# A new order of all steps, and another choice of the steps that GpSimd takes, in a gated-attention kernel with two feed-forward layers

## The chip, the cores and the metric

The kernel runs on one core of one Trainium2 chip. The metric is the device time of one execution in microseconds (us). The engines are named as in the profile: PE is TensorE, DVE is VectorE, ACT is ScalarE, POOL is GpSimd, SP is SyncE, which here does nothing but issue DMAs.

## The reference

```python
def _attn_ref(q, k, v, f_logit):          # (4, 8, 768, 48) each
    f = 1.0 / (1.0 + np.exp(-f_logit))
    state = np.zeros((B, H, D, D))
    for t in range(S):
        state = f[:, :, t, :, None] * state + np.einsum('bhd,bhe->bhde', k[:, :, t], v[:, :, t])
        y[:, :, t] = np.einsum('bhd,bhde->bhe', q[:, :, t], state)
    return y
# x = y as 3072 tokens of 384
def _moe_ref(x, w_a, w_b, w_out):         # 384 -> 1536 -> 384
    return ((x @ w_a) * (x @ w_b)) @ w_out
def _moe2_ref(x, w1, w2, w3, w_out):      # 384 -> 768 -> 384
    h = np.maximum(np.maximum(x @ w1, x @ w2), x @ w3)
    return h @ w_out
```

All arrays are drawn in double precision for the weights and single precision for q, k, v and f_logit; the output is single precision.

## The kernel before

The 3072 tokens are cut into 12 segments of 256 (three for each batch entry). Each segment goes through three kinds of work.

1. The attention's products inside groups of eight tokens are done with elementwise steps on DVE or POOL (`direct_steps`, kind "d", lines L200 to L254, three of them reductions that only DVE does: L203, L212 and L231), with a few copies and the sigmoid on ACT (kind "c"). Then `attn_steps`: small transposes and matmuls on PE (kind "P", in this order: total, transposes of k and q, the output of the groups, state keys, state update, state read, and twice scores and scores by values), tables on DVE or POOL (kind "g", L291 to L300), scalings, state decays and gains and the masks (kind "h"), copies out of PSUM on ACT (kind "b"). `x_out` (kind "x") brings the segment's result with ten DMAs into the layout of the next layer.
2. The first layer, `moe1_steps`. Every product is made of three matmuls of a high and a low part. A step "m" is nine matmuls of 128x256 (one 128-row tile of x @ w_a or x @ w_b), a step "y" nine matmuls of the down product. After each pair of tiles ACT copies the a half out of PSUM (L479), DVE multiplies it by the b half (L483, `v_ab`), ACT rounds it (L487), DVE takes the low part (L492, `v_g`, "gl"), and then two steps "y" (L502) can run.
3. The second layer, for six blocks of 512 tokens: steps "u" (`up2`, nine matmuls of 128x512, L646), copies and maxima on ACT and DVE (kinds "N" and "M"), steps "o" (`down`, three matmuls of 128x384, L672), then a copy and a store ("O", "X").

The weights arrive as double precision and are turned into a high and a low part on the chip, unit by unit of 128x384 (`conv_steps`). There are 36 units for the first layer and 24 for the second. A unit is loaded by SP (kinds "r" and "W"), read by two ACT instructions (L544, L545), shifted by DVE (L550), added by POOL (L554, always POOL), rounded by ACT (L561) and subtracted by DVE or POOL (L566). A step "m" needs the three units of its 384 columns, a step "y" its own unit.

Nothing is scheduled by the compiler. The steps are put into queues by kind, and the string `ORDER` names, letter by letter, which kind's next step is emitted:

```python
    with tc.manual_schedule():
        todo = {kind: iter(steps) for kind, steps in queues.items()}
        for kind in ORDER or CANON:
            f, args = next(todo[kind])
            f(*args)
```

Each engine carries out its own steps in that order and waits, by semaphores, for what a step reads or overwrites. So a step that waits holds up everything behind it on its engine, and SP's DMAs too wait for each other in the order of the letters. There are 2775 letters. The steps that either engine can do are numbered (0 to 643) in the order in which they are put into the queues, and the set `ON_POOL` says which of them POOL takes; DVE does the others:

```python
    def flex(kind, f):
        e = pool if len(FLEX) in ON_POOL else vec
        FLEX.append(len(CANON))
        step(kind, f, e)
```

Of the kernel before, what the change touches and what calls it, by code (L numbers as in the profile page):

```python
# [16 lines left out]


ORDER = (
    "zqzjckzrd0drd0vdddirdddr1tddddrddrcd0dP1drr12br2ddgd3Pgcd2b3kP4jgbd0hdgdgr13dg020dgdd4qd1ggdhbrrd01b"  # L20
    "4hhgP341P0hbh1Ph2hh32hrhPc204h1ldd3dr34h2bdr2d4P030h3Pdv14dr4t10Pd23h20d1122Pbd43b01dd01xd4ddrc3xddd"
    "sd2P2bdrddd3ggcgge4dPbsrP0dde1srem20brkmgdjm34r1db4dhg0q3g2ddg1nhrbdr0g34grmh1P4f320hmnP34f0mm2yhhb"
    "Pr10n43h0m2rrh1y34fm2hmn043f0nd1m12mrhyryhh3l23c141h4f20103m2rbPhrn3m4P014fm1021rr342hn3023Pd4Pm1h2m"
    "0y23fr34y40dn11044mvf1y23d2d0d01r324ynP34b41ddx0mdmf22mdnfdmm3dxn413mdy2yf3nds4f4sedddysecebyPddnPdb"
    "mcmgdngmgdddmdgtdbknfqgmndPmfbbmhymdgnmdhdgbgdymdfnmPjchgdfhghPnbmhfymhvldPhmdnhfhmdydbdhdnhhmfhnmd"
    "dddPdPhmPdfPdhmPdcbdntmyddPxdPmddfbcgxydmmbndqdymyddPdggsdfndsggsgeeyebgfdkjmnddyYmfbybdhmchgynnPhhP"
    "mdghgdnfbmPnhfmdbhdyhdmhdhymhhnhfddmPPmnmflhPdPhvmdddndmdcyfdnmdddPmydcdfbmdtnbdPbjfPgddbmnydmdmgkc"
    "PfdhmddgdnfmymbqxmdbdyndbgdxmvfgsdYesesyyglenfnmhdyggfmgyhPPmbyhhdPdhmgnhdhnnmhdhmfbndmfymddnhhhdct"
    "ddddmPdhPfjdcqhdynmkmPfPddnmmYhddyfPdncmbfmddPddPddmnbbgdfxdbggdydmPxPggngyhbmmbbggyfhmnhhdhfPgvdbd"
    "ynmPymhgmhfhndybhdhhdhhmdslhdedyPfsnesPdefmcymyhddmdPPnmnnhddfdtmPnfdmbncddjddmPbPybhddmfcmykdgmdmnd"  # L30
    "gfnPdddgqmdgmyfddnfdbmndmddgymmymgfmxgbhdgnyfbldndhmvhmYymPxfddgddPnfmydnhbmshPfysdsdbeeenmdyhcmfgd"
    "jhdhhymhhhtyPcdPhnnmnddmPfkPdhnmfmPmnmydmfmbPnPfddndmdcmfddymdqmbyndmfndmbdgdymdfgmbyxngxmhfdngdmdf"
    "dgymvnmydYgdgmyfngddhPdcsdssePeyedblmfdybdmgnbfdjhghkymyndnPnmbmbhcPdhhdfhdnhfqhdmmhhndhhymPdPdfmdyc"
    "hmPnPddmfynmhdPbdddfdmydmdddbnmYPfPvmbddndbmgfndfdyghmmgdggPddxnPgmddyfdbbmygmmbxndydfncmsshgdfdesey"
    "eymnfcdymtjhdynhmPkmdqddcnngbddmhgfhbhnfPhmdmnhhydmmhdhhhdfPPdhlnfdmmdPPddhndmfmPdmybmPndbddYgfdvPd"
    "ngtybmgmydxPdgfyggnhdbmxyghfgbmdggbhPnPhmmhycdhmbPfmydmnhfhbydnhchshdhflhssnededePdPyhdmPfdjqdPdymy"
    "dnhmnddPmnkdYmcdddfbbxPnbddPmfbmPdgdnmgmgggfdnghbbybgmgdfdhymnhymmfnhxytdgdhmmdPgPfmdhndbfmnfdPhdvm"
    "mnymfcmyhmhhhnhdcmldymftbdhsnyedPhsfPnsyeehmyPPfymdhPymbbPPnmbnndgddmdbdfYndPmfghbmdgybgndgmmfnymdxm"
    "fyggnmmlhfbndyfmghmPPgnhxmymfyhnmmbfynmgmPfhnhyhmmfhyhnhhmshyfnebPfsshePehmymymnPnPmYhnmPfmnfbnmxym"
    "fnxmwyfmmnmfmWynWmmymfnAABmfBynWCAfBmWAnDmCymWfmnCBfWWEymAmDymCAnsDssyDfnyeBeemfymyWmWEnCnBnAmDEECDB"  # L40
    "AfWWnmCmBAWfEBmpECyADmnfWnCBmymDDEEACfWmyGGmnWmyDfEBnWfHGmWAmWACEHBnCDyBmHmDpuAuyWBNCfDAumCBnWmDfEuE"
    "nWACuMDyMmBNfEnNAACmuDMEMWAyfmnMmymByEfYCnuNBfCMDyuEABEWDyCAonDBnoBuACoDouENCMGWoAuMBEoCDNEBooAEMGuN"
    "MoHBMuDEoNCDEouCHuDGoHMoNMouuoMuNoMNoMMuooouNEMuNuMoMOoopNXuOMoGuHNXoOoMuMOoNuuGMooNMuMuouNMooHXNoMu"
    "ooGMNouMXNMuMHuoooNuoNMuoMoMuNouoMNooOuMoopOMuONuuXOMNoMouMGXoHoNuMoNMuXMuGuuNooHoNMooMoGuMoNMoXoHoN"
    "uMuMuNoMNuuoMpMGoNuoGMouooOouOYNMMNuXuouMXoNMOMouOouNoMNouMuMooNoHNMuMuoMouooNuuuMoGNHoXMHMooNuuMouX"
    "pNMoMouoNMoOouuGoONMoMOuNuMoHNOuMMGoNooMoooNuHuMMuNuuMoouoNMMuXuooNuXMoGNuXHMMoooNMNuouMXMuoooNMNuuo"
    "ouMOMoNuOouMNoOooMMONouuNMXuoMMXuNMouooNouMMoooNMouooNuMMuNouNMuooMMNooMoXOXoXoOoXOXOX"
)


ON_POOL = {
# [12 lines left out]
}  # L64

CANON = []
# [744 lines left out]
```

## Time and profile before

| what | value |
|---|---|
| median of 3 runs | 971.65 us (971.62 to 972.44) |
| the profiled execution | 970.14 us |
| its span, from the first to the last instruction | 968.4 us |
| PE, PEld (weight loads) busy | 903.6 us (93%), 837.8 us |
| DVE, ACT, POOL busy | 573.3 us, 336.0 us, 305.0 us |
| mean granted TensorE clock | 0.995 |

The profiled execution took 1.7 us more than its span, and the median of the runs lies 1.5 us above the profiled execution. PE's busy time is the union of its matmuls, so that what is missing to the span (64.8 us) is time in which no matmul ran. A busy time on DVE and POOL runs from the start of an instruction to its end, and takes in time in which the instruction was held up on the way.

### The profile page before, as it was taken

The page shows a single profiled execution, that of the slowest core. Times are in us where ns is not written, and L with a number is a line of the kernel's source. Part 1 is how long each engine was busy: PE and PEld are TensorE (multiplying, and loading weights), DVE is VectorE, ACT ScalarE, POOL GpSimd, SP SyncE. Part 2 cuts the span into 40 slices and gives each one's busy share as a digit, 9 for nine tenths or more (in the row PEclk, how much of TensorE's full clock was granted, in tenths as well). Part 3 has the DMA queues.
Part 4 walks back from the last instruction along what each step waited for, and adds up shares of the span by engine and source line. Part 5 has one row for each costly group of instructions (what it writes and reads, how often), then busy time and mean ns, then how long its engine had stood idle before and what let it go on. Part 6 is the DMA issues. An engine that isn't in the chain of part 4 may idle for free.

```text
span 968.4 us, 22900 instructions
## 1 busy us (share of the span) xinstructions
PE 903.6 (93%) x9860; PEld 837.8 (87%) x9860; DVE 573.3 (59%) x893; ACT 336.0 (35%) x640; POOL 305.0 (31%) x297
## 2 busy tenths in 40 slices
PE   1348989999999999999999999999999999999998
PEld 0338889999999999999999999999888888888887
DVE  7999988977877857678765432464522232323221
ACT  4456742423324323242342323564421212112121
POOL 3543637464365336443263300462400000000000
PEclk9999989999999999999999999999999999999999
DMA  8446021322224221231220104261110110100000
GB/s 300 153 161 273 7 78 59 123 76 71 90 64 124 67 75 34 64 119 42 78 91 18 58 2 159 80 226 45 33 44 12 44 49 20 35 28 17 1 32 34
DMA packets 36294, 74.72 MB, mean 77 GB/s; under 512 B 5344, under 2 KB 17760, under 8 KB 36192
## 3 DMA queue, kind: packets, MB, share of 16 engines
q1 hardware_dynamic: 36192, 73.25, 22.3%
q8 instruction: 77, 1.26, 0.6%
q14 instruction: 25, 0.20, 0.1%
HBM read 59.07 MB, written 9.44 MB: 71 GB/s over the span
## 4 chain that ended last, share of the span: by engine, by line
PE 85%; DVE 9%; DMA 2%; SPq 1%; issue 1%; ACT 1%; POOL 0%; DVEq 0%; ACTq 0%; POOLq 0%
PE p L646 23%; PE pb L473 15%; PE pa L473 15%; PE y L502 15%; PE y L672 4%; PE pa L672 2%; PE pb L672 2%; PE w L275 2%; PE o L395 2%; PE o L365 2%; PE w L378 2%; PE w L337 1%; DMA kn<-in_k_dram 1%; DVE gl L492 1%; DMA ub<-in_moe_w_b_dram 1%
## 5 line engine op out<-in xcount | busy, mean ns | idle before, releaser
L473 PE MATMUL pb<-xh,ub 128*128 128x256 f32 x864 | 166.0, 288 | 1.4 <-DVE ub L566 0.9
L473 PE MATMUL pa<-xh,ua 128*128 128x256 f32 x864 | 167.0, 290 | 0.0
L502 PE MATMUL y<-gh,uo 128*128 128x256 f32 x864 | 164.6, 286 | 1.5 <-ACT gh L487 0.9
L646 PE MATMUL p<-ub,u 128*128 128x512 f32 x486 | 165.9, 395 | 0.0
L502 PEld LDWEIGHTS y<-gh,uo 128*128 128x128 f32 x864 | 135.9, 193 | 3.4 <-ACT gh L487 1.1
L473 PEld LDWEIGHTS pa<-xh,ua 128*128 128x128 f32 x864 | 136.8, 195 | 2.1
L473 PEld LDWEIGHTS pb<-xh,ub 128*128 128x128 f32 x864 | 134.8, 192 | 4.4 <-DVE ub L566 1.3
L473 PE MATMUL pa<-xl,ua 128*128 128x256 f32 x432 | 123.8, 287 | 2.1 <-DVE xl L464 2.1
L502 PE MATMUL y<-gl,uo 128*128 128x256 f32 x432 | 123.4, 286 | 2.5 <-DVE gl L492 2.5
L473 PE MATMUL pb<-xl,ub 128*128 128x256 f32 x432 | 122.3, 283 | 0.0
L646 PEld LDWEIGHTS p<-ub,u 128*128 128x128 f32 x486 | 90.5, 188 | 19.1
L646 PE MATMUL p<-ua,u 128*128 128x512 f32 x324 | 101.8, 395 | 0.0
L487 ACT CAST gh<-a 128x512 fp32r<-128x512 f32 x72 | 44.6, 619 | 139.1 <-DVE a L483 118.1
L483 DVE TENSOR_TENSOR a<-a,pb 128x512 f32<-128x512 f32 x72 | 49.2, 683 | 73.1 <-PE pb L473 71.3
L473 PEld LDWEIGHTS pa<-xl,ua 128*128 128x128 f32 x432 | 84.0, 195 | 2.8 <-DVE xl L464 2.7
L502 PEld LDWEIGHTS y<-gl,uo 128*128 128x128 f32 x432 | 83.5, 193 | 3.1 <-DVE gl L492 3.1
L656 DVE TENSOR_TENSOR uo<-uo,p 128x512 f32<-128x512 f32 x36 | 24.8, 688 | 101.1 <-PE p L646 84.0
L473 PEld LDWEIGHTS pb<-xl,ub 128*128 128x128 f32 x432 | 82.9, 192 | 0.0
L479 ACT COPY a<-pa 128x512 f32<-128x512 f32 x72 | 42.5, 590 | 87.9 <-DVE gl L492 43.8
L492 DVE TENSOR_TENSOR gl<-a,gh 128x512 fp32r<-128x512 f32 x72 | 64.2, 891 | 12.8 <-ACT gh L487 12.7
L646 PEld LDWEIGHTS p<-ua,u 128*128 128x128 f32 x324 | 60.4, 188 | 11.7
L656 DVE TENSOR_TENSOR ua<-ua,p 128x512 f32<-128x512 f32 x36 | 24.8, 688 | 72.1 <-PE p L646 72.0
(206 smaller groups left out, 1558.7 us busy)
## 6 DMA issues: line engine op xcount, KB each, us to landing
vlev<-in_v_lev_dram SPq DMA_DIRECT2D x12, 576.0 KB, 4.4
u<-in_moe_w_dram SPq DMA_DIRECT2D x18, 384.0 KB, 5.4
uo<-in_moe_w_out_dram SPq DMA_DIRECT2D x14, 384.0 KB, 7.0
qn<-in_q_dram SPq DMA_DIRECT2D x12, 384.0 KB, 3.8
fn<-in_f_logit_dram SPq DMA_DIRECT2D x12, 384.0 KB, 3.2
kn<-in_k_dram SPq DMA_DIRECT2D x12, 384.0 KB, 3.6
ua<-in_moe_w_a_dram SPq DMA_DIRECT2D x12, 384.0 KB, 6.2
vn<-in_v_dram SPq DMA_DIRECT2D x12, 384.0 KB, 3.9
```

What stands on the lines that cost most here:

```text
L275: mm(pair[0][h], lhsT=pair[1][h], rhs=ident[half(h), half(h)], is_transpose=True, start=first_of_bank(n), stop=True, skip_group_check=True)
L365: mm(os_[0][64 * hl:64 * hl + D, hi // 2, o:o + 64], lhsT=st[64 * hl:64 * hl + D, c, hi * D:hi * D + D], rhs=qv[64 * hl:64 * hl + D, hi, c ...
L378: mm(w[half(hl ^ hp), hp, i, 64 * lev:64 * lev + 64], lhsT=KL[lev][ps, o:o + 64], rhs=rhs, start=True, stop=True, skip_group_check=True)
L473: mm(ps, lhsT=col(w, i, j, h), rhs=x2[x][:, i], start=(n == 0), stop=(n == 3 * KC - 1), skip_group_check=True)
L479: act.copy(out=g2[jj][0], in_=ps2["a"])
L483: vec.tensor_mul(out=a, in0=a, in1=ps2["b"])
L487: act.copy(out=g2[jj][1], in_=g2[jj][0])
L492: vec.tensor_sub(out=g2[jj][2], in0=a, in1=gh.bitcast(F32))
L502: mm(ps, lhsT=wts["o", j][:, w, m * P:m * P + P], rhs=g, start=(j == 0 and n == 0 and m != 1), stop=(j == NJ - 1 and n == 2), skip_group_c ...
L646: mm(ps, lhsT=col(n, i, f, w), rhs=y, start=(c == 0), stop=(c == 3 * KC - 1))
L656: vec.tensor_max(out=hset[k][0], in0=hset[k][0], in1=u_ps[b, f, n])
L672: mm(o_ps[t], lhsT=h[:, t * P:t * P + P], rhs=wts[down_units[f]][:, w], start=(f == 0 and n == 0), stop=(f == NF - 1 and n == 2))
```

## The change

The letters of `ORDER` are put into another order. It has the same 2775 letters, so the same steps. `ON_POOL` becomes another set, of 246 numbers where it had 226. Nothing else is touched: tiles, pools, instructions and their shapes are the same. In the diff, cut to the head and the last lines of the order and the head of the set:

```diff
 ORDER = (
-    "zqzjckzrd0drd0vdddirdddr1tddddrddrcd0dP1drr12br2ddgd3Pgcd2b3kP4jgbd0hdgdgr13dg020dgdd4qd1ggdhbrrd01b"
-    "4hhgP341P0hbh1Ph2hh32hrhPc204h1ldd3dr34h2bdr2d4P030h3Pdv14dr4t10Pd23h20d1122Pbd43b01dd01xd4ddrc3xddd"
-    "sd2P2bdrddd3ggcgge4dPbsrP0dde1srem20brkmgdjm34r1db4dhg0q3g2ddg1nhrbdr0g34grmh1P4f320hmnP34f0mm2yhhb"
-    "Pr10n43h0m2rrh1y34fm2hmn043f0nd1m12mrhyryhh3l23c141h4f20103m2rbPhrn3m4P014fm1021rr342hn3023Pd4Pm1h2m"
-    "0y23fr34y40dn11044mvf1y23d2d0d01r324ynP34b41ddx0mdmf22mdnfdmm3dxn413mdy2yf3nds4f4sedddysecebyPddnPdb"
...
-    "pNMoMouoNMoOouuGoONMoMOuNuMoHNOuMMGoNooMoooNuHuMMuNuuMoouoNMMuXuooNuXMoGNuXHMMoooNMNuouMXMuoooNMNuuo"
-    "ouMOMoNuOouMNoOooMMONouuNMXuoMMXuNMouooNouMMoooNMouooNuMMuNouNMuooMMNooMoXOXoXoOoXOXOX"
+    "zzzrvqkji0rl1t23d4cdr01d2d3dr04d1d2d3r04d1d2dr0ddc13dc4dr02d31k4d2PPr0db3b1q4jdggPgr02bg1hd3b4cdgbdr"
+    "0gdgh1d2r0dg3dghghdr0hd1d1vd0r4d1d2PPd3r0hb1dbP4rd0t2hdh312hr43h042hPd314r0dhd12hPdr02h31P34dP42dr0h"
+    "23P134dlb4rd0x2bcd31dc4dr02xsd3e4d1PPd02dbrb2qk3Pgjhs43eb4drsbe0dm1bd1mdcgdm2nr0md23md3fgdmn4r01fmdn"
+    "m1dyr02fvynd31mfdyr04dm14dPngydr0g2mg13mhg4mr0g2fnmh3mfhnr4P0hygb1hybg1Pr0h2mt132hmh32frhn43h0f2hy43"
+    "ryh012hP134dPr042hd4P3Pr04m12hmnd31P2r0l4b123xb432m043m1fdmn4fmxdn2md3dys4fdynfsdysecdyecdedmnndmYdm"
...
+    "HGMuNHuMuMNMuuuooOoOXoOoNoOMoMoXuNNMoXMooouXuMNMuNoMooouuMNMuNuMuMNMuuuoooooNoMuMNMuuoooNoOMuOXMNMuX"
+    "uooOoOXoNoMuMNXMuuooNoMuMNMuuoooNoMuMNMuuoooNoMuMNMuoooNoMoMoNMooOoOXoOOXXX"
 )
...
 ON_POOL = {
-    39, 44, 88, 148, 149, 155, 161, 162, 163, 164, 166, 168, 169, 171, 172, 173, 174, 175, 178, 181,
...
+    0, 27, 29, 30, 35, 37, 42, 51, 65, 66, 67, 69, 72, 81, 83, 107, 115, 135, 137, 147, 150, 157,
+    159, 165, 166, 170, 172, 173, 175, 179, 184, 185, 186, 187, 189, 190, 191, 196, 197, 200, 201,
...
 }
```

The numbers 0 to 35 are the last step (L566) of the 36 weight units of the first layer, 36 to 83 belong to segment 0, 84 to 132 to segment 1, 133 to 181 to segment 2.

## Rows read from the trace of the kernel before

**Rows 1.** The page's head: the span, and each engine's busy time (share) and instructions.
```profile
span 968.4 us, 22900 instructions
...
PE 903.6 (93%) x9860; PEld 837.8 (87%) x9860; DVE 573.3 (59%) x893; ACT 336.0 (35%) x640; POOL 305.0 (31%) x297
```

**Rows 2.** Busy time by stretches of 25 us (x instructions), granted clock, DMA.
```profile
core 0: us, PE busy (x) PEld busy (x) DVE busy (x) ACT busy (x) POOL busy (x), PEclk, DMA share, GB/s
0.00:25.00 25.00, 3.07 (x38) 2.36 (x38) 18.10 (x34) 11.69 (x23) 8.12 (x16) 1.00 0.84 301
25.00:50.00 25.00, 9.70 (x225) 8.55 (x229) 24.50 (x46) 11.88 (x25) 14.90 (x8) 1.00 0.36 137
...
100.00:125.00 25.00, 22.66 (x359) 21.13 (x354) 25.00 (x41) 17.37 (x36) 13.48 (x10) 1.00 0.06 16
125.00:150.00 25.00, 21.97 (x178) 20.83 (x178) 22.00 (x30) 9.99 (x20) 13.45 (x15) 0.86 0.32 105
...
200.00:225.00 25.00, 25.00 (x428) 23.99 (x427) 17.18 (x23) 9.39 (x16) 16.92 (x17) 1.00 0.31 98
```

**Rows 3.** Whom PE waited for from 135 to 960 us: total, times, longest.
```profile
PE y L502 <- DVE gl L492: 1.0, 2, 0.8
```

**Rows 4.** The timeline from 125 to 136 us: start, duration, instruction, idle time before it.
```profile
127.83 1.79 POOL L232 TENSOR_TENSOR op<-vn,sc 128x768 f32<-128x768 f32 x1
...
128.21 1.96 DVE L492 TENSOR_TENSOR gl<-a,gh 128x512 fp32r<-128x512 f32 x1
...
130.22 0.58 PE L502 MATMUL y<-gl,uo 128*128 128x256 f32 x1 [1.50 <-DVE gl L492]
```

**Rows 5.** Busy time by stretches of 5 us, columns as in Rows 2.
```profile
125.00:130.00 5.00, 2.19 (x14) 1.59 (x13) 5.00 (x5) 2.62 (x7) 4.45 (x3) 0.92 0.30 87
130.00:135.00 5.00, 4.78 (x34) 4.52 (x34) 4.97 (x10) 1.24 (x4) 0.20 (x2) 0.50 0.24 79
```

**Rows 6.** DVE's timeline from 24 to 36 us.
```profile
23.83 0.55 DVE L236 TENSOR_TENSOR prod<-vn,sc 128x384 f32<-128x384 f32 x1
24.30 0.21 DVE L294 TENSOR_TENSOR gt<-tt 128x32 f32<-128x32 f32 x1
...
25.28 0.35 DVE L242 TENSOR_TENSOR op<-op,prod 128x192 f32<-128x192 f32 x1
25.55 1.03 DVE L296 TENSOR_TENSOR gt<-gt,tt 128x32 f32<-128x32 f32 x1
...
29.10 0.96 DVE L252 TENSOR_TENSOR prod<-prod 128x768 f32<-128x768 f32 x1
```

**Rows 7.** DVE's timeline from 12 to 20 us.
```profile
12.81 0.95 DVE L212 TENSOR_REDUCE sc<-prod 128x16 f32<-128x768 f32 x1
...
17.44 0.24 DVE L228 TENSOR_TENSOR tp<-fn 128x96 f32<-128x96 f32 x1
```

**Rows 8.** POOL's timeline from 12 to 40 us.
```profile
12.71 1.05 POOL L215 TENSOR_TENSOR kn<-kn,fn 128x384 f32<-128x384 f32 x1 [2.21 <-DVE prod L208]
...
25.50 1.01 POOL L554 TENSOR_TENSOR cvt<-cvt,ub 128x384 int32<-128x384 int32 x1 [4.97 <-DVE cvt L550]
```

**Rows 9.** The timeline of the first 14 us.
```profile
4.75 0.84 ACT L199 ACTIVATE fn<-fn 128x768 f32<-128x768 f32 x1 [2.53 <-DMA fn<-in_f_logit_dram]
...
6.77 0.96 DVE L200 TENSOR_TENSOR prod<-qn,kn 128x768 f32<-128x768 f32 x1 [5.90 <-DMA kn<-in_k_dram]
...
7.67 0.55 ACT L544 ACTIVATE cvt<-ua 128x384 f32<-128x384 f32 x1 [2.07 <-DMA ua<-in_moe_w_a_dram]
```

**Rows 10.** The chain that ended last, from 440 to 475 us: start, duration, what.
```profile
445.09 1.26 PE pa L473 x9
446.36 1.08 PE pb L473 x9
```

**Rows 11.** Groups by line and shape: busy, mean ns, idle time before and releasers.
```profile
L483 DVE TENSOR_TENSOR a<-a,pb 128x512 f32<-128x512 f32 x72 | 49.2, 683 | 73.1 <-PE pb L473 71.3 <-ACT st L447 0.8 <-ACT q L429 0.5
L201 POOL TENSOR_TENSOR qn<-qn,fn 128x768 f32<-128x768 f32 x2 | 3.7, 1844 | 2.3 <-DVE prod L200 2.3
```

More of the change, by code (lines that the diff above doesn't have):

```diff
@@ L25 @@
[L25 to L44, printed above, removed]
@@ L45 @@
-    "uMuMuNoMNuuoMpMGoNuoGMouooOouOYNMMNuXuouMXoNMOMouOouNoMNouMuMooNoHNMuMuoMouooNuuuMoGNHoXMHMooNuuMouX"
-    "pNMoMouoNMoOouuGoONMoMOuNuMoHNOuMMGoNooMoooNuHuMMuNuuMoouoNMMuXuooNuXMoGNuXHMMoooNMNuouMXMuoooNMNuuo"
-    "ouMOMoNuOouMNoOooMMONouuNMXuoMMXuNMouooNouMMoooNMouooNuMMuNouNMuooMMNooMoXOXoXoOoXOXOX"
+    "zzzrvqkji0rl1t23d4cdr01d2d3dr04d1d2d3r04d1d2dr0ddc13dc4dr02d31k4d2PPr0db3b1q4jdggPgr02bg1hd3b4cdgbdr"
+    "0gdgh1d2r0dg3dghghdr0hd1d1vd0r4d1d2PPd3r0hb1dbP4rd0t2hdh312hr43h042hPd314r0dhd12hPdr02h31P34dP42dr0h"
@@ new lines @@
+    "23P134dlb4rd0x2bcd31dc4dr02xsd3e4d1PPd02dbrb2qk3Pgjhs43eb4drsbe0dm1bd1mdcgdm2nr0md23md3fgdmn4r01fmdn"
+    "m1dyr02fvynd31mfdyr04dm14dPngydr0g2mg13mhg4mr0g2fnmh3mfhnr4P0hygb1hybg1Pr0h2mt132hmh32frhn43h0f2hy43"
+    "ryh012hP134dPr042hd4P3Pr04m12hmnd31P2r0l4b123xb432m043m1fdmn4fmxdn2md3dys4fdynfsdysecdyecdedmnndmYdm"
+    "kdnddjPPbqmbgdmgfhPcgdmngbdmfbdmngbdgydgdgfhyndmhmfgydnyghmdhvmdmfndmdfPdnPybhbydhPdmhtdhmhdmhfdmhnh"
+    "dhPfdnPdyhdPPdyhdcPdcdmlbdmxddmdfndPPbmbgkjgmdqxfmdnhyfsdnyecfPdsybedysbebdmngdnmgYdgdmngdmhvmgdfnmf"
@@ new lines @@
+    "mgnhyyghghmdmdfPdnPfmbhbmndPdythdhyhdmhdmhdfhPdhnPfdmhmdndmcdPfcPdndmmfhdmndPmlbddkbmxfdPPbmgbggdmqj"
+    "PhxmbdbydsbeydcydnsyfsendyefgdynggdghmfmdydymngvdnnmYghmfdmnhdmfgPndPmbdbmfndPfmthdmnhmmdfdmhdmhdmhd"
+    "hydhydhhPcdnhdcfPdnyfhdmPdPdkdmhdjPqmlbdbmxddcPPdbdybgdgyhndfPxgnyggbdfygdnbmfbgdmhvmnggmhyghsfdssyn"
+    "eyfeyhedydmndnYPdPmbhbmnPdhdmtmhdfdmnhmdhfmdnhyfdhnmhdPfdhcdPdcyhdmdPnPdmhdkdPdjybqlyxddPPbcmgdbmgfd"
+    "mngdxgmdgfmghndyhdyfggndmgdmfvmdngyddmdmfnydmfmdnmdysfsseyndedPePbdmfbdbydhydhPndmnhbYmdchnbmcdmdfnm"
@@ new lines @@
+    "fmdndmdkddjmqmfdnPfmtchdnmdhmdhmdfhydhhPdhddPmhdPPdvmhyddPdnylbfbyxdnfmndmfmdnmxddmfdmddmdmdPPsbeysg"
+    "cdbyedsghPnPecgfbydnybfbgmgndmgfygdhkydgdyhjqygdgPnmnhbYdmnbchmfmdnhPfdmtnhmdhmdfmdnhdhmfhndmhdmfhdm"
+    "hvdmmddPddPdyhdPPdyhdPndfylbdnyxbfdPPndbmbgfmghdPnxgPcgdbmgdcmbdbmfgdmghmgmdgykhsssyededPnejybhdqgbh"
+    "yfPdncytfhnmfmdhmdhdmhydhdyhdhydhdPnnhnYdPfvdmnfmhdmndPdPmhdPfdmlbndmxmfdnmdmfdmxddmdmdyddPPbdybcygd"
+    "nfPPdbgykdcghbygndbmgfqjgmdngggmgfmhndmcmhydfydnhdmfdnmhdPsfsyhbsybndyefePdedythdmmhvdmhdmhdhdyhdPnn"
@@ new lines @@
+    "hndYPfdmnmhdmfdnPdPdmhdmdfmdnmdfmdndyfdmmmmPylbbyxnfPPbnygdbfggmcgdghnmgfxhyngggmgmmfmmmyssesePnePdb"
+    "yfcbdynbyhydPhmbdfhbmndfPdhytydmndnnmYhdmhfdmnhdmfdnyhdyhdhmhdhPfnfPmhPPyhPylbbmxPPnbmbggggggmghghPx"
+    "PfbmggnbmfbhynhPybhbmhmhPfnmhhfmhhyhnhhyPPmhmPfPnfmhmmnPmbyfssesyneefxmyymnnxmnmmfYnmfwmWnyyWAmBmfCn"
+    "mDfWAmEnByCyDWAEmBCmfnmDWfAmEnByCmDWAEyfBnmCmfWADmBnEmCWAmfDBmnEmfCWAmnBDyCfsssEyDeWAeEyneBmfCyWAyDB"
+    "EyCmDWnEAmnBmnYCmWAfDmBpnECmfDmAEynBfCWynDfmGEGyHWAHyGBCmHDmnWEApmBmCfnmAfmDWBnEyCGGyHDHGuWEAHBpCmND"
@@ new lines @@
+    "mAfEnmBCWmfDEmnyfWAynBmCfmDWAEynBCyDmWAEmBCufDnWEAfuMBCyWAMyNBDCunMDEnAYEoNoBoCouDEuMuMNMuNoMooouuMN"
+    "MuNuMuMNMuuuoooooNoMuMNMuoGoGHoGHoNHooMpuMNMuNuMoMoOoNXoOMOuOXoNooouXuMXuMNMuNoMooouuMNMuNoMooouuMNM"
+    "uNoMuuMNMuuoGoGHoGHoNHooMpoMuNMoNoOoOXoOuOXuMuXMNMuNXoMooouuMNMuNoMooouuMNMuNuMuMNMuuuoooooNoMuMNMuo"
+    "GoGHoGHuNHMpMuNMuuooooNoOMoOXMoOuNOMNXoMooouXuMXNMuNoMooouuMNMuNoMooouuMNMuNoMooouuMNMuNoMooouuMGGHN"
+    "HGMuNHuMuMNMuuuooOoOXoOoNoOMoMoXuNNMoXMooouXuMNMuNoMooouuMNMuNuMuMNMuuuoooooNoMuMNMuuoooNoOMuOXMNMuX"
```

22 rows, old and new, of the table ON_POOL are left out of this document.

## The prediction

> **What bounds the kernel now.** I read the head of the page first: PE is busy for 903.6 of 968.4 us, so 64.8 us of the span have no matmul [rows 1]. The stretches of 25 us say where they lie. PE is busy for 3.07 us of the first stretch and for 9.70 of the second, for 22.66 of the stretch from 100 and 21.97 of the one from 125, and for all of the one from 200 [rows 2]. Summed over all stretches, 60 of the 64.8 us lie ahead of 200 us, 3.9 in the last 18 us (copy and store of the last block) and 0.8 near 600. The waits of PE from 135 to 960 us confirm it: the costliest comes to 1.0 us in all [rows 3]. From 200 us on the kernel is the sum of its matmuls, and the order of steps can only add to that.
>
> Ahead of 135 us another engine sets the pace. DVE is busy for 24.50 of the 25 us from 25 and all of those from 100 [rows 2]. The last wait of this phase is plain in the timeline: step "y" eleven of segment 0 stands for 1.50 us until 130.22, for the low part gl of the sixth pair, on which DVE worked from 128.21 for 1.96 us [rows 4]. PE was busy for 2.19 of the 5 us from 125, and in the next 5 us its granted clock was 0.50, the lower of its two levels (1.2 of 2.4 GHz) [rows 5]. From there PE catches up with nobody: if one adds up its steps at their pace in the steady part (1.08 us for nine matmuls, 1.26 behind an attention step [rows 10]), time less sum is 78.9 us when segment 1's first "y" starts, and it then grows only by the price of the switches between the two kinds of work. **So the time is: when does DVE release PE, and does PE wait again afterwards.**
>
> **The change, part by part.** I went through both orders letter by letter and put against each step of PE the steps of DVE and POOL that it needs, and all that stands ahead of those on their engines.
>
> *DVE's own work.* Ahead of the gl of 130.2 us DVE has 213 instructions in the old order and 194 in the new, while PE has the same 54.0 us of steps ahead of the "y" that waits. The balance of 19 is 22 that leave and 3 that come. At the fastest duration of each kind (0.55 us for 128x384, 0.96 for 128x768, 0.35 for 128x192, 0.21 for a table [rows 6]) the 22 are worth 9.9 us and the 3 1.6: **-8.3 us**. Instructions of DVE start some 0.08 us before the one ahead is shown as ended (L294 at 24.30, while L236 runs from 23.83 for 0.55 [rows 6]); 19 fewer such overlaps give **+1.5**.
>
> *What POOL's share costs DVE.* 18 of those 22 have gone to POOL (four last steps of weight units, six tables, two decays, six others), and up to that gl POOL has 56 instructions where it had 40. They are dearer there: L201 takes 1.84 us on POOL, a DVE instruction of this size 0.96 [rows 6, 11]. And they are not free for DVE. L296, a table of 0.21 us, lasts 1.03 when it starts 0.05 us behind a POOL instruction that runs from 25.50 to 26.51, and ends with it [rows 6, 8]. I compared each of DVE's 893 instructions with the fastest of its kind: 107 are longer by over 0.15 us, 72.6 us together, and every one of them started beside a running POOL instruction and ended its own time after that one's end. From 25 to 125 us the excess is 16.4 us over 33 POOL instructions, 0.50 each; over the whole trace it is 0.25 each (72.6 over 287). A reduction is not held: L212 keeps its 0.95 beside a POOL instruction of 1.05 [rows 7, 8]. The 16 more lie in the phase in which DVE has no gaps, so I take 0.50: **+8.0 us**. From below it is nothing (all of them beside reductions or gaps); from above DVE loses their whole own time, 14.2 less 3.0 us for what leaves POOL, 11.2.
>
> The Trainium skill has this as a rule (SBUF — State Buffer, section Who interferes with whom): a DVE instruction with two inputs in SBUF and a GpSimd instruction that reads SBUF exclude each other for the whole instruction, whichever comes second waits, and a reduction takes no part. The trace agrees in all three points. Taken literally it would put the bound of 11.2 us in place of 8.0, and the sum 3.2 us higher.
>
> *The start.* The old order loads q, f and k first: the sigmoid starts at 4.75, the first product at 6.77 with the third load, the first weights' step at 7.67 with the fourth [rows 9]. The new one begins with a weight unit and v, so k is fourth and f fifth. A load of 384 KB takes about 1 us there, so DVE's first product starts near 7.7, the sigmoid ends near 9.5, and the product with it is on POOL for 1.84 us [rows 11], with the next DVE step behind it. Each further unit (three columns of weights are turned ahead of the attention's total) then passes ACT, DVE, POOL, ACT and DVE in turn. Laid end to end at the fastest durations, L228, which releases PE's first transpose, ends near 24.3 us instead of 17.68 [rows 7]. Of these 6.6 us 3.5 are DVE work that has only moved forward (already in the sums above); the other **+3.1** are lost. From below 1.0 (the later load alone), from above 5.
>
> *Sum at the gl that releases PE:* -8.3 + 1.5 + 8.0 + 3.1 = +4.3 us, with bounds of -5.8 and +9.4. At the next places the balance is alike: the first step "m" of segment 1 has 9.1 us less DVE work, 16 more POOL instructions and 1.0 us more of PE's work ahead.
>
> *The clock.* The low clock from 130 us cost about 3 us (half speed for some 6 us). The new order gives PE fewer holes in this phase, since segment 0's matmuls start later and lie closer. I take half: **-1.5**, bounds 0 and -3.
>
> *Later waits.* The new order leaves PE less to do while others answer. Between the second "b" tile of one pair and the first of the next lie only two steps (2.16 us) in 24 of 60 places, where it was 3; L483 with 0.683 us has to fit in there behind whatever DVE is at [rows 11]. And in 10 places, where it was 3, only one step lies between scores and scores by values, which just covers the mask: before, such a place cost some 0.1 us. I take **+1.2** for both (0.7 masks, 0.5 the rest), from below nothing, from above 8 (a third of a microsecond at each of the 24).
>
> *What costs nothing.* Number and switches: 76 changes from attention to tiles instead of 78, 0.18 us each, **-0.4**. In the second layer longer rows of "u" and of "o" replace the finer mixture; at least two "u" (4.2 us) lie between the last "u" of a tile and its first "o", which covers the chain of three short steps between them; at the very end 3.2 us stand there instead of 2.1. The units of the second layer are loaded as late as before, counted in PE's steps. SP: more weights (20 instead of 16) stand ahead of segment 0's output DMAs, so fewer are held behind them; that helps ACT, which is not the bound.
>
> **Sum.** 4.3 - 1.5 + 1.2 - 0.4 = +3.6 us. The profiled execution took 970.14 us, so it would take 973.7; the median of the runs lies 1.5 above it: **975.2 us**.
>
> **The rivals.** What a measurement of this kernel can tell from no change is about 0.2%, 1.9 us.
>
> 1. *Faster: POOL's extra steps find DVE's gaps.* One mechanism at one place, the gl of segment 0's sixth pair. At the price of the whole trace, 0.25, the 16 cost 4.0 instead of 8.0, so DVE releases PE at +0.3, and PE without the long hole keeps its clock (-3): -3.1 us in all, 968.5. At no price 964.5. It decides as soon as a POOL instruction costs DVE less than about 0.3 us there. For it: over the whole trace that is the price, and the small tables are short. Against it: the price in this phase is 0.50.
> 2. *It doesn't do what an order can do.* PE is full from 200 us either way, and with a sum between -1.9 and +1.9 nothing is to be seen: 971.6. For it: gain and loss at the gl are of one size.
> 3. *Much slower: the short distances in the first layer bite.* If half of the 24 places cost 0.5 us each, 6 us come on top: 981. For it: DVE is busy for 17.18 of 25 us there, POOL has more in hand and holds it [rows 2]. Against it: only 1.0 us of such waits is seen now, with three such places [rows 3].
>
> **How the numbers follow.** My forecast (slower by 2 to 7 us) has 0.35, rival 1 0.31, rival 2 0.21, rival 3 0.13. Faster 0.31, same 0.21, slower 0.48. The range runs from 964.5 (rival 1 at no price) to 982 (rival 3 and a little); below it lies a start that loses nothing too, above it the whole 8 us of later waits. The forecast's own range is 973.6 to 979.
>
> **What would show it.** In the new profile PE's first transpose should start near 24 us; DVE should be full until about 134 us with its excess beside POOL near 25 us for that phase; the sixth gl should end near 134; PE should be full from then on but for waits for L483, L492 and L383 that come to 1 to 2 us. A gl that ends before 130 us makes the forecast wrong on the fast side, PE waits of over 4 us after 140 on the slow side, and a start near 18 us would show that the order of the loads doesn't matter.

## The result, and the profile after

The changed kernel takes 979.12 us (median of four executions, 977.79 to 980.97), the kernel before 972.01 us beside it (971.62 to 972.44). The ratio is 1.0074, 95% interval 1.0055 to 1.0093: **slower by 7.1 us**, where 3.6 were forecast. The time lies in the stated range (964.5 to 982) and just above the forecast's own (973.6 to 979). The profiled execution took 979.89 us with a span of 978.1, 9.7 more than the span before.

The head of the page, which answers to [rows 1]:

```profile
span 978.1 us, 22888 instructions
...
PE 902.4 (92%) x9860; PEld 836.8 (86%) x9860; DVE 573.6 (59%) x873; ACT 340.0 (35%) x640; POOL 328.6 (34%) x317
```

PE's matmuls take 1.2 us less than before; 75.7 us of the span have none, 10.9 more than before. The stretches of 25 us, columns as in [rows 2]:

```profile
0.00:25.00 25.00, 0.00 (x0) 0.00 (x0) 15.47 (x26) 12.16 (x24) 12.39 (x20) 1.00 0.58 216
25.00:50.00 25.00, 6.91 (x130) 5.80 (x130) 24.25 (x40) 13.29 (x26) 11.41 (x11) 1.00 0.54 190
...
125.00:150.00 25.00, 24.46 (x219) 23.66 (x219) 22.85 (x40) 13.41 (x27) 11.76 (x12) 1.00 0.29 102
150.00:175.00 25.00, 23.10 (x424) 22.10 (x423) 18.24 (x26) 5.35 (x9) 12.26 (x11) 0.93 0.11 33
175.00:200.00 25.00, 23.26 (x251) 22.24 (x250) 19.96 (x26) 10.34 (x18) 14.57 (x15) 1.00 0.37 120
...
250.00:275.00 25.00, 23.45 (x446) 22.32 (x445) 20.41 (x24) 4.31 (x9) 15.58 (x12) 0.93 0.21 66
```

PE starts later and has less done by 50 us, but the hole near 130 us and the low clock behind it are gone (24.46 of 25 us at 1.00, against 21.97 at 0.86 [rows 2]). What is new stands later: holes of 1.5 to 1.9 us at 150, 195 and 265 us, and a clock of 0.93 in two of these stretches. Whom PE waited for from 135 to 960 us, where [rows 3] had 1.0 us for gl:

```profile
PE y L503 <- DVE gl L493: 2.8, 2, 1.9
PE pa L474 <- ACT a L480: 2.3, 2, 1.3
PE pb L474 <- DVE a L484: 0.9, 1, 0.9
```

(All line numbers are one higher than before.) The timeline at the three places, other rows between them left out:

```profile
149.15 2.39 POOL L248 TENSOR_TENSOR prod<-vn,sc 128x768 f32<-128x768 f32 x1 [1.03 <-DVE op L243]
150.12 1.96 DVE L493 TENSOR_TENSOR gl<-a,gh 128x512 fp32r<-128x512 f32 x1
152.14 0.39 PE L503 MATMUL y<-gl,uo 128*128 128x256 f32 x1 [1.90 <-DVE gl L493]
...
196.75 1.97 POOL L427 TENSOR_TENSOR kt<-kt,gt 128x1024 f32<-128x1024 f32 x1
197.50 1.77 DVE L493 TENSOR_TENSOR gl<-a,gh 128x512 fp32r<-128x512 f32 x1 [0.69 <-ACT gh L488]
199.32 0.39 PE L503 MATMUL y<-gl,uo 128*128 128x256 f32 x1 [0.88 <-DVE gl L493]
...
262.57 3.74 POOL L220 TENSOR_TENSOR prod<-qn,kn 128x768 f32<-128x768 f32 x2 [1.62 <-DVE qn L217]
264.53 2.33 DVE L493 TENSOR_TENSOR gl<-a,gh 128x512 fp32r<-128x512 f32 x1
266.89 0.58 ACT L480 COPY a<-pa 128x512 f32<-128x512 f32 x1 [3.58 <-DVE gl L493]
267.53 0.50 PE L474 MATMUL pa<-xh,ua 128*128 128x256 f32 x2 [1.30 <-ACT a L480]
```

It is the picture of [rows 4] three times: a gl of 0.68 us lasts 1.77 to 2.33 because a POOL step runs beside it, and PE stands. At 265 us the "y" had cover enough, but ACT may not overwrite a before gl has read it, so the next tile waits instead. At 195 us the gl is only half of it (0.88 of 1.74 us). The other 0.87 comes ahead of it, at the product a (L484), which stands on DVE behind a table step (L298) that lasts 1.85 us beside POOL's L253, and 0.20 in only_195, where L253 is on DVE:

```profile
193.99 2.16 POOL L253 TENSOR_TENSOR prod<-prod 128x768 f32<-128x768 f32 x1 [1.82 <-DVE prod L248]
194.36 1.85 DVE L298 TENSOR_TENSOR a<-ft,tt 128x32 f32<-128x32 f32 x1
196.87 0.50 PE L474 MATMUL pb<-xh,ub 128*128 128x256 f32 x2 [0.87 <-DVE a L484]
```

And of the 2.3 us in the row "pa" 1.0 is no held gl: at 357 us ACT's copy stands behind the sigmoid, which had waited for the load of f.

```profile
356.55 0.84 ACT L200 ACTIVATE fn<-fn 128x768 f32<-128x768 f32 x1 [2.46 <-DMA fn<-in_f_logit_dram]
357.92 0.50 PE L474 MATMUL pa<-xh,ua 128*128 128x256 f32 x2 [1.00 <-ACT a L480]
```

The three places of 150, 195 and 265 us in stretches of 5 us, columns as in [rows 5]:

```profile
150.00:155.00 5.00, 3.10 (x20) 2.90 (x19) 4.12 (x5) 0.59 (x1) 3.95 (x3) 0.83 0.07 14
155.00:160.00 5.00, 5.00 (x37) 4.92 (x35) 1.89 (x4) 0.62 (x1) 0.80 (x1) 0.83 0.19 68
195.00:200.00 5.00, 3.26 (x25) 2.85 (x24) 4.31 (x4) 1.21 (x2) 4.70 (x4) 1.00 0.24 74
265.00:270.00 5.00, 3.45 (x58) 3.04 (x62) 3.42 (x3) 0.58 (x1) 4.04 (x4) 0.94 0.24 76
270.00:275.00 5.00, 5.00 (x131) 4.66 (x124) 3.18 (x3) 0.59 (x1) 0.00 (x0) 0.72 0.53 167
```

Summed over all stretches of 5 us, with 5 less PE's busy time as hole and (1 less the clock) by 5 as what the clock lacked:

| | holes to 140 us | clock to 140 | holes 140 to 960 | clock 140 to 960 |
|---|---|---|---|---|
| before | 59.6 | 5.1 | 1.4 | 0.0 |
| after | 65.5 | 0.0 | 6.8 | 3.4 |
| difference | +5.9 | -5.1 | +5.4 | +3.4 |

Together +9.6, the 9.7 of the spans: up to 140 us only +0.8, the rest behind it. (The 5.1 before are the 3.4 near 130 us [rows 5] and 1.7 at 80 us, where the clock was 0.66.) The +0.8 is a low value: in the seven other profiled executions below that have this opening and these engines in it, holes and lost clock to 140 us come to 66.3 to 68.7 us, against 64.7 before. So the opening costs 1 to 4 us.

### The profile page after: what moved, and what is told of

Its sections match the earlier page's. It is cut to its first block, busy times and chain, and to the rows that moved or that the text cites. A ratio compares the mean times of both kernels' runs of the same rounds, so it can differ in the third digit from the quotient of the medians.

```text
span 978.1 us, 22888 instructions
## 1 busy us (share of the span) xinstructions
PE 902.4 (92%) x9860; PEld 836.8 (86%) x9860; DVE 573.6 (59%) x873; ACT 340.0 (35%) x640; POOL 328.6 (34%) x317
## 4 chain that ended last, share of the span: by engine, by line
PE 81%; DVE 10%; DMA 3%; ACT 2%; issue 2%; SPq 2%; POOL 1%; DVEq 0%; ACTq 0%; POOLq 0%
PE p L647 23%; PE y L503 14%; PE pa L474 14%; PE pb L474 13%; PE y L673 4%; PE o L396 2%; PE pa L673 2%; PE pb L673 2%; PE w L379 2%; PE w L276 2%; PE o L366 2%; PE w L338 1%; DMA ub<-in_moe_w_b_dram 1%; SPq L412 1%; DMA ua<-in_moe_w_a_dram 1%
## 5 line engine op out<-in xcount | busy, mean ns | idle before, releaser
L474 PE MATMUL pa<-xh,ua 128*128 128x256 f32 x864 | 164.1, 289 | 2.3 <-ACT a L480 2.3
L474 PE MATMUL pb<-xh,ub 128*128 128x256 f32 x864 | 163.3, 287 | 1.7 <-DVE a L484 0.9
L484 DVE TENSOR_TENSOR a<-a,pb 128x512 f32<-128x512 f32 x72 | 49.2, 684 | 63.1 <-PE pb L474 51.7
L493 DVE TENSOR_TENSOR gl<-a,gh 128x512 fp32r<-128x512 f32 x72 | 68.2, 947 | 29.7 <-ACT gh L488 29.1
```

Of the source, the lines that this page charges most:

```text
L474: mm(ps, lhsT=col(w, i, j, h), rhs=x2[x][:, i], start=(n == 0), stop=(n == 3 * KC - 1), skip_group_check=True)
L484: vec.tensor_mul(out=a, in0=a, in1=ps2["b"])
L493: vec.tensor_sub(out=g2[jj][2], in0=a, in1=gh.bitcast(F32))
```

## The experiments

**The theory:** the opening is nearly paid for by the clock, and the time is lost in the middle, where POOL steps hold a gl. **The rival:** the late start and POOL's extra work in the opening cost it. Times below are medians, and each ratio is against the kernel before on the same chip (970.65 us for runs 1 to 4, 969.87 for run 5, 970.94 for runs 6 and 7, 971.19 for run 8), so the differences count and not the bare times. "left(order, part)" stands for an order without as many letters of each kind as the part has; letter 537 of the changed order, and 532 of the old one, counted from 0, is the first "y" of segment 1. The two parts hold the same steps but for four of "d" and "g" and a few others.

**1. open_new**: the changed opening, the old rest.

```diff
-ORDER = new
+ORDER = new[:537] + left(old, new[:537])
+# ON_POOL: the new set for the steps of the first part, the old set for the others
```

> The changed kernel's steps up to the first y of segment 1 (near 140 us), with the engines it chose for them, and the kernel before's order and engines for all that is left. Theory (the lost time lies in the middle, where POOL steps stretch a gl on DVE and PE waits, with the clock falling after it): the changed opening costs 0.5 to 2.5 us, so 972.5 to 975. Rival (the later start, first transpose 26.1 instead of 17.7, and the POOL work of the opening cost the time): 977 to 981.

976.32 us, ratio 1.0053 (1.0038 to 1.0068): +5.1. Neither range holds it. The seam makes a wait of its own: the old rest hands both L248 to DVE just then, and PE stands 2.43 us at 154 us,

```profile
PE pb L474 <- DVE a L484: 2.4, 1, 2.4
```

and in the profiled execution the clock fell twice (1.7 us each, at 110 and at 155 us). It says nothing of the opening alone.

**2. open_old**: the old opening, the changed rest.

```diff
-ORDER = new
+ORDER = old[:532] + left(new, old[:532])
+# ON_POOL: the old set for the steps of the first part, the new set for the others
```

> The other half: the kernel before's steps and engines up to the first y of segment 1, the changed order and engines for all that is left. Theory (loss in the middle): 976 to 981, with the waits of y for gl near 150, 195 and 265 us still there. Rival (loss in the opening): 971 to 974.

974.75 us, ratio 1.0047 (1.0030 to 1.0063): +4.6. The bare time lies between the two ranges. The holes from 140 to 960 us come to 4.6 us, where the kernel before has 1.4; near 195 and 265 us PE still stands (1.6 us each), at 150 us no more. So the changed rest costs 3 to 6 us without the changed opening, seam included. This and the next run carry the theory, not the first.

**3. late_engines_old**: the changed order, but the old choice of engines from segment 1 on.

```diff
-ON_POOL = new_set
+ON_POOL = {n of new_set in new[:537]} | {n of old_set in the rest}
```

> The changed order throughout, the changed choice of engines up to the first y of segment 1, and from there the kernel before's choice of the steps that GpSimd takes. If the choice makes the loss in the middle: 971 to 975, the three long waits for gl gone or others in their place. If the order makes it: 977 to 982.

972.15 us, ratio 1.0014 (1.0006 to 1.0023): +1.4. The largest waits that are left from 135 to 960 us:

```profile
PE y L503 <- DVE gl L493: 0.7, 2, 0.5
PE o L276 <- POOL op L255: 0.4, 1, 0.4
```

**The choice of POOL's later steps costs 5.7 of the 7.1 us; the new order, with its engines in the opening, the other 1.4.**

**4. five_on_dve**: of all those steps only the five beside the three places.

```diff
-ON_POOL = new_set
+ON_POOL = new_set - {157, 208, 223, 290, 291}
```

> The changed kernel, with five steps taken from POOL and given to DVE in their own places: the L248 beside the gl at 150 us, the L253 and the L427 beside the two-step place at 194 to 199, and the two L220 beside the gl at 264. Theory (a POOL step beside a gl stretches it by 1.1 to 1.6 us, PE waits, the clock falls): the gl come back to 0.7 us, the waits of 1.9, 1.7 and 1.5 us go and with them the falls of the clock (3.4 us in all), DVE has 5 us more to do where it has gaps: 970.5 to 975. Rival (DVE is late there whoever takes these steps, and 5 us more on DVE are paid by PE): 978 to 984.

972.99 us, ratio 1.0025 (1.0017 to 1.0034): +2.4, so five of 246 numbers are worth 4.7 us. The holes from 140 to 960 us fall from 6.8 to 1.3 us (the one at 357 us goes too: the sigmoid there now runs ahead of the copy), and the five steps cost DVE nothing that PE sees.

**5. The five one place at a time** (only_150, only_195, only_265), three kernels.

```diff
-ON_POOL = new_set
+ON_POOL = new_set - {157}          # only_150
+ON_POOL = new_set - {208, 223}     # only_195
+ON_POOL = new_set - {290, 291}     # only_265
```

> The changed kernel with one step given from POOL to DVE: the L248 beside the gl at 150 us. Theory: its wait (1.9 us) shrinks to about 0.5 and the fall of the clock behind it (1.7 us) goes, so 3 us less than the changed kernel: 975 to 977. Rival (a wait taken away there comes back at the next place): 978 to 980.

> The changed kernel with two steps given from POOL to DVE: the L253 and the L427 beside the steps at 194 to 199 us. Theory: the wait there (1.7 us) goes, no fall of the clock stood behind it: 977 to 978.5. Rival (DVE's own 2 us more are paid there): 979 to 981.

> The changed kernel with the two L220 beside the gl at 264 us given from POOL to DVE. Theory: the wait of 1.5 us goes, and the fall of the clock behind it (1.7 us): 975 to 977. Rival (DVE's own 1.9 us more are paid there): 979 to 981.

977.55, 977.87 and 976.74 us, ratios 1.0078, 1.0077 and 1.0077 (each about 0.0015 either way). Against the 1.0074 of the changed kernel none shows a gain. only_150 misses its theory by the bare time too; the other two meet it only because the kernel before is 2.1 us quicker on that chip. The traces do show each wait go: the hole of the stretch from 150 us shrinks from 1.90 to 0.81, that from 195 from 1.74 to 0.12, that from 265 from 1.55 to nothing. In only_150 the gl is back at 0.68 us and PE still waits 0.81, for DVE's steps ahead of it:

```profile
151.05 1.21 DVE L427 TENSOR_TENSOR kt<-kt,gt 128x1024 f32<-128x1024 f32 x1
152.18 0.68 DVE L493 TENSOR_TENSOR gl<-a,gh 128x512 fp32r<-128x512 f32 x1
152.92 0.39 PE L503 MATMUL y<-gl,uo 128*128 128x256 f32 x1 [0.81 <-DVE gl L493]
```

Over all stretches from 140 to 960 us less is gained at 150 us: the holes come to 6.4, 5.2 and 4.7 us, against 6.8, so in only_150 most of what goes there comes back at later places, as its rival said. Such gains of 0.4 to 2.1 us the interval hides, the more so as the fall of the clock, which I had added to two of them, turned out to be loose: in only_150 the holes at 195 and 265 us stayed (3.21 and 3.43 of 5 us busy) and the clock of every stretch to 960 us was 1.00.

**6. memset_beside**: is it any POOL instruction that holds gl, or one that reads?

```diff
-ON_POOL = new_set
+ON_POOL = new_set - {157}
+            # in segment 2, at that step's place:
+            for _ in range(3):
+                pool.memset(prod[:, 0:16], 0.0)
```

> The changed kernel, with the L248 that ran on POOL beside the gl of 150 us given to DVE, and in its place on POOL three memsets of the 128x768 elements that it wrote (some 2.2 us at 0.9 us for 128x960). Nothing is read by them. If any POOL instruction holds a DVE instruction of two inputs: the gl takes 1.5 to 2 us again and y waits over 1 us there. If only POOL instructions that read hold it: the gl takes 0.7 us, and y waits for it at most 0.6 us there. In both cases the two later places, at 195 and 265 us, stay as they are: 975 to 979.

978.03 us, ratio 1.0076 (1.0063 to 1.0089). The memsets run through the gl and don't touch it (the added lines shift the line numbers):

```profile
149.72 2.34 POOL L251 MEMSET prod<- 128x768 f32 x3 [1.01 <-DVE op L243]
150.72 0.68 DVE L499 TENSOR_TENSOR gl<-a,gh 128x512 fp32r<-128x512 f32 x1
151.45 0.39 PE L509 MATMUL y<-gl,uo 128*128 128x256 f32 x1 [0.36 <-DVE gl L499]
```

So at this place it is not POOL's being busy that costs, but its reading. The Trainium skill says so (SBUF — State Buffer, section Who interferes with whom): a DVE instruction with two inputs in SBUF contends with a GpSimd instruction that reads SBUF, and not with one that only writes. The trace agrees: 0.68 us beside memsets, 1.96 beside a product of 2.39 us, where the memsets take 2.34.

**7. The opening** (all_engines_old, loads_first, old_engines_loads_first): three kernels with the changed order.

```diff
-ON_POOL = new_set
+ON_POOL = old_set                      # all_engines_old and old_engines_loads_first
...
-ORDER = "zzzrvqkji0rl1t" + new[14:]
+ORDER = "zzzqjkrvi0rl1t" + new[14:]    # loads_first (ON_POOL of run 3) and old_engines_loads_first
```

> The changed order with the kernel before's choice of engines throughout: against the run that has the old choice only from segment 1 on, 13 steps of the opening go back from POOL to DVE. Theory of the forecast (such a step costs DVE about as much on POOL, by holding a DVE instruction, as on DVE itself): within 1.5 us of that run, 970.5 to 973.5. Rival 1 (POOL relieves DVE, which sets the pace there): 975 to 979. Rival 2 (POOL's steps cost DVE more than their own time): 966 to 970.

> The run with the changed order and the old choice of engines from segment 1 on, and one thing more: at the very start q, f and k are loaded ahead of the first weight unit and of v, as the kernel before does. The forecast gave the late start a price of 3.1 us (1 to 5). If that is right: 1 to 3 us less than without the edit, so 969 to 971. Rival (the opening is ruled by what DVE does later, a start 2 us earlier only gives DVE a gap): 971.5 to 973.

> Both edits at once: the changed order, the old choice of engines throughout, and q, f and k loaded first. If the two add: the time of the run with the old engines less the gain of the loads, 967 to 972. If the later start was already covered by the longer DVE work, no more than the better of the two.

all_engines_old: 973.06 us, ratio 1.0024 (1.0015 to 1.0033). Against the third run 22 steps go back from POOL to DVE and 8 the other way, 14 fewer on POOL (the text above has 13). That changes 1.0 us, as expected there, and the two intervals overlap. loads_first: 974.42 us, ratio 1.0046 (1.0032 to 1.0060), **3 us worse** where a gain was expected by the one and nothing by the other. Both edits: 976.16 us, ratio 1.0050 (1.0036 to 1.0065), where 967 to 972 was expected. The reason is on ACT, in late_engines_old first, then in loads_first:

```profile
4.03 0.54 ACT L545 ACTIVATE cvt<-ua 128x384 f32<-128x384 f32 x1 [1.80 <-DMA ua<-in_moe_w_a_dram]
9.31 0.84 ACT L200 ACTIVATE fn<-fn 128x768 f32<-128x768 f32 x1 [2.66 <-DMA fn<-in_f_logit_dram]
24.85 0.55 DVE L228 TENSOR_TENSOR kp<-kn,fn 128x384 f32<-128x384 f32 x1
```

```profile
8.18 0.54 ACT L545 ACTIVATE cvt<-ua 128x384 f32<-128x384 f32 x1 [5.95 <-DMA ua<-in_moe_w_a_dram]
11.29 0.84 ACT L200 ACTIVATE fn<-fn 128x768 f32<-128x768 f32 x1
27.02 0.54 DVE L228 TENSOR_TENSOR kp<-kn,fn 128x384 f32<-128x384 f32 x1
```

In the changed order the first weight unit stands ahead of the sigmoid on ACT. With q, f and k loaded first that unit comes 4.15 us later and the sigmoid, whose data are there, waits behind it. L228 is 2.17 us later, the sixth gl 1.9 and the end of the span 2.5: here the delay of the start was paid about in full.

**8. before_two_on_dve**: the lesson put to the kernel before, at the wait of [rows 4].

```diff
-ON_POOL = old_set
+ON_POOL = old_set - {148, 149}
```

> The kernel before, in its own order, with two steps of segment 2 given from POOL to DVE: the L230 and the L232 that run on POOL from 126.2 to 129.6 us beside the L566 of 1.35 us and the gl of 1.96 us for which y waits there (rows 4). On DVE they stand behind that gl. Theory (it is the POOL step beside the gl that costs, in the kernel before too): the gl comes back to 0.7 us and ends about 2 us earlier, the wait of 1.5 us goes, and the low clock behind it (about 3 us) may go as well: 965 to 969.5. Rival (PE stood there for other reasons, gh and the earlier steps of DVE; 1.7 us more on DVE are paid at the next place): 970 to 973.

**966.78 us, ratio 0.9959 (0.9945 to 0.9972): 4.0 us faster than the kernel before**, and the only kernel here that beats it. The gl, and the stretches that answer to [rows 5]:

```profile
128.18 0.68 DVE L492 TENSOR_TENSOR gl<-a,gh 128x512 fp32r<-128x512 f32 x1
128.92 0.38 PE L502 MATMUL y<-gl,uo 128*128 128x256 f32 x1 [0.22 <-DVE gl L492]
```

```profile
125.00:130.00 5.00, 3.89 (x30) 3.45 (x29) 5.00 (x10) 2.75 (x8) 1.03 (x1) 1.00 0.35 100
130.00:135.00 5.00, 4.86 (x53) 4.59 (x52) 5.00 (x9) 3.08 (x6) 0.80 (x3) 1.00 0.47 128
```

The wait falls from 1.50 to 0.22 us, and the low clock behind it is gone. The mean granted clock of its five executions is 0.9972, that of the nine of the kernel before beside them 0.9947: of the 4 us about 2.4 are the clock (0.0025 of 967). In the two profiled executions it is more: 3.4 us of clock and 0.7 of holes to 140 us.

## Why the prediction came out as it did

The direction and the range held, and the mechanism, a POOL step that holds DVE, is the one that was named. But it was priced in the opening, and most of the time was lost behind it; the sum was 3.5 us short. For the opening the forecast was +2.8 (4.3 - 1.5), and runs 3 and 4 leave 1.4 and 2.4; for what follows it was +0.8 (1.2 - 0.4), and the rest, 5.7 or 4.7, lies there.

- **DVE's own work and POOL's share** (-8.3, +1.5, +8.0: together +1.2). Right as an exchange: all_engines_old shows that 14 steps more or fewer on POOL are worth about 1.0 us. The size of POOL's term was too large. Compared with the fastest of its kind, DVE's instructions from 25 to 125 us were over by 19.1 us, counted as the 16.4 before, where near 25 was forecast. (The price of the whole trace, 0.25, leaves out what is below 0.15 us, and POOL has 297 instructions [rows 1], not 287; counted alike it is 0.27, and nothing hangs on that.)
- **The start** (+3.1, bounds 1 and 5). The mechanism was right, the size at its upper bound:

```profile
24.91 1.06 DVE L229 TENSOR_TENSOR tp<-fn 128x96 f32<-128x96 f32 x1
26.07 0.37 PE L276 MATMUL o<-ident,tp 64*128 64x64 f32 x2 [26.07 <-DVE tp L229]
```

  The release comes at 25.97 instead of the forecast 24.3, 8.3 us behind the 17.68 of before [rows 7]; less the 3.5 that only moved, 4.8 are lost, 0.8 of it because L229 itself was held (1.06 us, where [rows 7] has 0.24). In the other seven executions with this opening the transpose starts 0.3 to 1.2 us later still.
- **The sum at the sixth gl** (+4.3, near 134 us). It ended at 133.09:

```profile
132.41 0.67 DVE L493 TENSOR_TENSOR gl<-a,gh 128x512 fp32r<-128x512 f32 x1
```

  +2.9 against 130.17 [rows 4]; in the other seven executions with this opening it ends at 133.9 to 135.2, so the forecast lies in their midst. The terms in the trace, over all of DVE's instructions ahead of it: own work -8.2, held by POOL +5.3, overlaps +1.9, and +5.1 of idle time, 2.6 of it ahead of 18 us and 3.7 behind 60 us, where DVE was to be full; the gl itself is 1.3 shorter than the held one of before. So POOL's term was too large, the gaps of DVE behind 60 us and the gl were left out, and that the sum fits is in part luck.
- **The clock** (-1.5, 0 to -3). Under-sized. The old opening lacked 5.1 us of clock, 1.7 of it at 80 us, which I hadn't seen; the new one none here, and 1.7 us in two of the other seven. Over all executions the kernel before has a mean granted clock of 0.9948 (60 executions; 5.1 us of 971), the changed one 0.997, 1.000, 0.998 and 0.998 (1.7 us of 979). That gave back 3.4 us, beyond the bound of 3; without it, by this estimate, the change would have cost over 10.
- **Later waits** (+1.2, bound 8). This is the term that failed: the holes from 140 to 960 us grew by 5.4. I had looked in the letters for short distances between PE's steps and at DVE's own queue, and priced L483 and the masks. What came was for the most part L493 held by POOL; 0.9 us came at L484 (the old L483), behind a held table, 0.3 at a mask, and 1.0 at ACT's sigmoid. I had worked that mechanism out for the opening, with a gl held in that way among the rows [rows 4], and then used it only ahead of 135 us, because DVE has gaps behind it. A gap elsewhere doesn't help: it needs one POOL step beside the one gl that PE is about to wait for. Five steps did 4.7 of the 7.1 us (run 4), and over 4 us of waits after 140 us was the sign named for the slow side.
- **What costs nothing** (second layer, SP): nearly nothing of it is seen; the holes from 300 to 960 us are 1.6 us, before 0.8. The 1.0 at 357 us, where a load came late for the sigmoid, is the exception.

The held steps at the three places are shown as the cause together (runs 3 and 4, and the waits in the traces). What each place is worth in time is open: singly none could be told from nothing. Open too is how the order's own cost divides between start and POOL. It is larger than the 1.4 us of run 3: the mean granted clock there is 0.9994, so 0.6 us lacked where the kernel before lacks 5.1, and with the clock set aside the order costs about 6. The opening with q, f and k first and the sigmoid moved with them wasn't tried.

## What to carry to other kernels

When work is moved to GpSimd, don't price it by sum or mean: list the few DVE instructions that PE waits for next, and look which GpSimd step can run beside each. Two steps taken away from such a place made the kernel before 0.4% faster, though GpSimd then did less and DVE more. And a load moved forward gains only if the engine that uses it reaches it earlier; the order of the loads and the order of their readers must move together.

## What the hardware showed that I had not expected

A hole in PE's work of one size costs different amounts from one execution to the next. The stretch from 265 us, with 3.45 of 5 us busy, was followed by a clock of 0.72 in the changed kernel; in only_150 the same stretch, 3.43 of 5 us busy, kept 1.00, and so did the next:

```profile
195.00:200.00 5.00, 3.21 (x25) 2.81 (x25) 4.31 (x5) 0.70 (x2) 4.70 (x4) 1.00 0.30 82
265.00:270.00 5.00, 3.43 (x76) 2.95 (x72) 3.84 (x4) 0.58 (x1) 4.46 (x4) 1.00 0.18 45
```

A fall in the middle cost about 1.7 us each time (the 0.83 of two stretches at 150 us, the 0.94 and 0.72 at 265 us). By the mean granted clock the four executions of the changed kernel lack between nothing and some 3 us (1.000 to 0.997), those of the kernel before between 3 and 7 (0.997 to 0.993). A small gain can't be read from one profile before that is set aside.
